# Splitting two weight loads and moving one unit's k^T v forward in the head of a fused retention + mixture-of-experts kernel

## Chip, cores, metric

One NeuronCore of one Trainium2 chip. The metric is the device time of one execution in microseconds (us). The kernel before took 535.12 us in the three runs that came with it (534.94 to 535.67). A line "L576" in a profile is line 576 of that kernel's source. Engines: PE is TensorE, DVE is VectorE, ACT is ScalarE, POOL is GpSimd, SP is SyncE.

## The reference

```python
# q, k, v: (8 batches, 8 heads, 576 positions, 64); w1: (4, 512, 1024); w2: (4, 1024, 512)
scores = q @ k^T / 8                                # per batch and head
ret    = scores * gamma_h ** (i - j)  for i >= j    # decaying causal mask
x      = (ret @ v)  ->  (4608, 512)
out    = sum over 4 experts of  p_e * (relu(x @ w1[e]) @ w2[e])     # p: row-normalised probabilities
```

The kernel computes the retention in chunks of 128 positions (with a remainder chunk of 64). Within a chunk it is a masked product (s, then sT, then o). What comes from earlier chunks is carried as a state k^T v of 64x64 per head (PSUM tile kvp, copied into the SBUF tile sbd).

## The kernel before

The first batch begins with four "units", numbered from 0 (two chunks, that is 256 positions, by 4 heads each). What matters is that each goes through these steps, and that units 1, 2 and 3 follow each other closely in the first 20 us:

```python
def trans_pe(self, between=0):     # PE: 8 transposes into pt; ACT: qkT <- pt   (qkT: a pool of 2 buffers)
    ...
    nc.scalar.activation(self.qk..., pt..., Copy)
def scores(self):                  # PE: 16 small matmuls s <- qkT; DVE: sT <- s * mask
def kv(self):                      # PE: kvp <- k^T v
    kvp = ring_tile("kvp0", [128, 2, 2, 128])
    if hf == 1 and self.carry is None:
        for g in range(2): mm(g, 128, slice(0, 2), 0)   # "prefix", the four 256-wide matmuls
    for g in range(2): mm(g, 128, 1, hf)
    for g in range(2): mm(g, 64, 0, hf)
    ...
    nc.scalar.activation(dst, src, Copy)                # ACT: sbd <- kvp, two of them
def values_own(self):              # PE: o <- sT, v      ("own o")
def values_carried(self):          # PE: o += qkT, sbd   ("carried o"); ACT: xt <- o, two copies

for u in range(NU):
    cast_unit(u + 2)               # ... (the last unit has a part of the first up product ahead of it)
    us[u].values_own()
    us[u + 1].scores()
    us[u].values_carried()
    us[u + 2].trans_pe(1)          # 1: one filler matmul w between the k and the q transposes
    us[u + 1].kv()
```

After this, from about 18 us, come the matmuls of the experts: up products (ph, from xt and w1) and down products (po, from h and w2), first for expert 0. Expert 0's w1 is loaded in two transfers of 512 KB, its w2 in one of 1 MB, all on GpSimd's queue.

## Time and profile before

| | kernel before |
|---|---|
| time, median of 3 | 535.12 us |
| span of the profiled execution | 533.5 us |
| PE busy | 526.2 us, 99% |
| DVE, ACT, POOL busy | 68%, 16%, 28% |
| granted TensorE clock | 1.00 throughout |
| k^T v of unit 1 starts / of unit 3 starts | 12.00 / 16.96 us |

The page's own chain of waits, which is followed back from the last instruction to whatever released each step, is made of PE almost alone (columns: engine, share of the span):

```profile
PE 73%; ACT 2%; DVE 0%; issue 0%
```

In the timeline, a row is a group of instructions of one kind: start, duration, engine, line, operation, out<-in, tile of the PE array, shape, count, and in brackets the idle time just before it and what ended that. The prediction shows the rows of the head.

### The profile page before, as it was taken

The page shows a single profiled execution, that of the slowest core. Times are in us where ns is not written, and L with a number is a line of the kernel's source. Part 1 is how long each engine was busy: PE and PEld are TensorE (multiplying, and loading weights), DVE is VectorE, ACT ScalarE, POOL GpSimd, SP SyncE. Part 2 cuts the span into 40 slices and gives each one's busy share as a digit, 9 for nine tenths or more (in the row PEclk, how much of TensorE's full clock was granted, in tenths as well). Part 3 has the DMA queues.
Part 4 walks back from the last instruction along what each step waited for, and adds up shares of the span by engine and source line. Part 5 has one row for each costly group of instructions (what it writes and reads, how often), then busy time and mean ns, then how long its engine had stood idle before and what let it go on. Part 6 is the DMA issues. An engine that isn't in the chain of part 4 may idle for free.

```text
span 533.5 us, 10230 instructions
## 1 busy us (share of the span) xinstructions
PE 526.2 (99%) x4260; PEld 342.0 (64%) x4260; DVE 361.4 (68%) x456; ACT 85.9 (16%) x175; POOL 146.8 (28%) x189
## 2 busy tenths in 40 slices
PE   8999999999999999999999999999999999999997
PEld 4644544478745985478646865587548844884486
DVE  5436768895577667697578767776765567557763
ACT  4723440012101111020101101100110000000010
POOL 5743104235235334235132514153000000000000
PEclk9999999999999999999999999999999999999999
DMA  9999947867778866736353666454010111110001
GB/s 241 198 217 245 244 122 191 166 154 163 150 166 155 176 142 148 153 83 162 108 135 94 144 139 114 104 118 126 20 41 25 56 39 41 41 41 20 1 24 56
DMA packets 144510, 63.55 MB, mean 119 GB/s; under 512 B 123728, under 2 KB 135264, under 8 KB 144464
## 3 DMA queue, kind: packets, MB, share of 16 engines
q1 hardware_dynamic: 134080, 43.42, 36.1%
q0 software_dynamic: 10240, 19.35, 16.2%
q8 instruction: 33, 0.54, 0.4%
q10 hardware_dynamic: 144, 0.13, 0.1%
q14 instruction: 13, 0.11, 0.1%
HBM read 53.56 MB, written 9.51 MB: 118 GB/s over the span
## 4 chain that ended last, share of the span: by engine, by line
PE 73%; ACT 2%; DVE 0%; issue 0%
PE ph L357 37%; PE pd L469 34%; ACT xt L290 2%; PE o L282 1%; PE o L277 1%; PE py L469 1%; DVE h L363 0%; PE or L342 0%; PE sr L336 0%; PE or L344 0%; DVE ob L497 0%
## 5 line engine op out<-in xcount | busy, mean ns | idle before, releaser
L357 PE MATMUL ph<-xt,w 128*128 128x512 bf16 x1136 | 250.9, 379 | 0.8 <-DVE h L363 0.2
L363 DVE SCALAR_TENSOR_TENSOR h<-ph,pB 128x1024 bf16<-128x1024 f32 x128 | 156.3, 1223 | 58.1 <-PE ph L357 57.2
L357 PEld LDWEIGHTS <-w 128*128 128x128 bf16 x1136 | 109.9, 98 | 127.9
L469 PEld LDWEIGHTS <-h 128*128 128x128 bf16 x1024 | 100.0, 98 | 13.4
L469 PEld LDWEIGHTS <-s 128*128 128x128 bf16 x768 | 75.0, 98 | 8.7
L469 PE MATMUL pd<-wx,h 128*128 128x256 bf16 x512 | 61.1, 273 | 0.2
L469 PE MATMUL pd<-wx,s 128*128 128x256 bf16 x512 | 61.1, 273 | 0.0
L218 POOL DMA_DIRECT2D pB<-pd x28 | 15.7, 562 | 151.7 <-DVE h L363 150.8
L504 POOL TENSOR_TENSOR ob<-v,p 128x256 f32<-128x256 f32 x15 | 11.8, 784 | 111.8 <-DVE v L501 83.8
L237 POOL TENSOR_TENSOR bf_k<-raw_k,gk 128x512 bf16<-128x512 f32 x24 | 26.1, 1088 | 36.6 <-DMA raw_k<-in_k_dram 23.2
L269 DVE TENSOR_TENSOR sT<-s,tri 128x1024 bf16<-128x1024 f32 x24 | 28.2, 1218 | 6.4 <-PE s L267 6.4
L290 ACT ACTIVATE xt<-o 128x768 bf16<-128x768 f32 (+6 forms) x24 | 13.0, 594 | 116.8 <-PE o L282 116.8
L469 PE MATMUL pd<-t4w,h 128*128 128x256 bf16 x256 | 30.6, 273 | 0.0
L442 DVE TENSOR_TENSOR s<-s,h 128x1024 bf16<-128x1024 bf16 x32 | 29.9, 973 | 0.0
L392 PE MATMUL po<-wx,h 128*128 128x512 bf16 x128 | 29.1, 379 | 0.0
L469 PE MATMUL pd<-t2w,s 128*128 128x256 bf16 x240 | 28.7, 273 | 0.0
L469 PE MATMUL pd<-t3w,h 128*128 128x256 bf16 x240 | 28.6, 273 | 0.0
L477 ACT ACTIVATE p<-pd 128x256 f32<-128x256 f32 x16 | 6.1, 383 | 138.8 <-PE pd L469 106.2
L237 POOL TENSOR_TENSOR bf_q<-raw_q,gq 128x512 bf16<-128x512 f32 x24 | 26.6, 1109 | 5.0 <-DMA rawr_v<-in_v_dram 2.1
L446 DVE TENSOR_TENSOR s<-h,s 128x1024 bf16<-128x1024 bf16 x32 | 26.4, 863 | 0.0
L440 DVE TENSOR_TENSOR s<-h 128x1024 bf16<-128x1024 bf16 x32 | 23.7, 779 | 0.0
L486 DVE TENSOR_TENSOR u<-pd,p 128x256 f32<-128x256 f32 x15 | 6.4, 424 | 22.4 <-PE pd L469 22.3
(160 smaller groups left out, 376.4 us busy)
## 6 DMA issues: line engine op xcount, KB each, us to landing
pB<-pd POOLq DMA_DIRECT2D x28, 256.0 KB, 3.6
raw_k<-in_k_dram SPq DMA_DIRECT2D x48, 128.0 KB, 2.6
raw_q<-in_q_dram SPq DMA_DIRECT2D x48, 128.0 KB, 2.9
raw_v<-in_v_dram SPq DMA_DIRECT2D x48, 128.0 KB, 3.3
wx<-in_moe_w_dram POOLq DMA_DIRECT2D x4, 1024.0 KB, 14.5
out_dram<-oa SPq DMA_DIRECT2D x16, 256.0 KB, 2.4
out_dram<-ob SPq DMA_DIRECT2D x15, 256.0 KB, 2.2
w<-in_moe_w_dram POOLq DMA_DIRECT2D x3, 1024.0 KB, 13.8
```

Source lines behind the costliest of these rows:

```text
L218: eng.dma_start(out=pB[t, e], in_=pd[e:e + 1, t * NT:(t + 1) * NT].to_broadcast([128, NT]))
L237: eng.tensor_tensor(bfs[p % 2][n], raw1[n], g[:, :, 2 * p:2 * p + 2].unsqueeze(3).to_broadcast([128, NC, 2, D]), op=MULT)
L269: nc.vector.tensor_tensor(sT[:, :, :, :].rearrange("p j c t -> p (j c) t"), s[:, :, :, :].rearrange("p j c t -> p (j c) t"), tri[:, :].uns ...
L290: nc.scalar.activation(xt_of(t)[:, self.ps, n0 + a - t * NT:n0 + z - t * NT], o[:, :, a:z], Copy)
L357: nc.tensor.matmul(ph[:, f, :], lhsT=w1_sb[e][:, dc, fc * 128:(fc + 1) * 128], rhs=x[:, dc, :], start=(dc == 0), stop=(dc == NDC - 1))
L363: nc.vector.scalar_tensor_tensor(h[:, fk:fk + 2, :], ph, 0.0, pB[t, e][:, :].unsqueeze(1).to_broadcast([128, 2, NT]), op0=MAX, op1=MULT)
L392: nc.tensor.matmul(po[:, g, :], lhsT=h[:, e * NFC + fc, ns * 128:(ns + 1) * 128], rhs=wx[e // 2][:, (e % 2) * NFC + fc, :, :].rearrange("p ...
L440: nc.vector.tensor_tensor(self.alloc("s1")[:, l], h[:, l, self.b], h[:, r, self.b], op=ADD)
L442: nc.vector.tensor_tensor(self.alloc("s2")[:, l], self.s1[:, l], h[:, l, self.a], op=SUB)
L446: nc.vector.tensor_tensor(self.alloc("s4")[:, l], h[:, r, self.a], self.s2[:, l], op=SUB)
L469: mm = nc.tensor.matmul(dst, lhsT=src[:, kk, tok], rhs=rhs(c), start=(start and c == 0), stop=(c == KH - 1), skip_group_check=True)
L504: nc.gpsimd.tensor_tensor(self.ob[:, HF:Dm], self.v, self.p5, op=ADD)
```

## The change

The intent has two parts. Smaller weight pieces let the first up and down products start with a part of the weights. And k^T v of unit 2 is used to fill PE's waits in unit 1: its prefix runs directly after unit 1's k^T v, into the second bank of the same PSUM tile; its other eight matmuls run before the carried o of unit 1, which used to wait for ACT. Its two state copies go from ACT to DVE, and the filler matmul between unit 3's transposes is dropped. The diff, cut to its core:

```diff
@@ the weights
-    load_w1_at = {1: (0, slice(0, F // 2)), 2: (0, slice(F // 2, F))}
+    load_w1_at = {1: (slice(0, F // 4),), 2: (slice(F // 4, F // 2), slice(F // 2, F))}
-    load_w2(0)
+    load_w2(0, 0, NFC // 2)
+    load_w2(0, NFC // 2, NFC)
@@ first down products of expert 0: fc 0-3 of two token blocks, then fc 4-7 of both
+        if e == 0 and m == 0:
+            todo = [(gg, fc) for gg in range(2) for fc in range(4 * g, 4 * g + 4)]
@@ kv(): tile of two banks, prefix on its own, copies
+                self.kvt = ring_tile("kvp0", [128, 2, 2, 2, 128])
-                    nc.scalar.activation(dst, src, Copy)
+                    self.reads.append(nc.vector.tensor_copy(dst, src) if others else nc.scalar.activation(dst, src, Copy))
@@ the loop over units
         us[u].values_own()
         us[u + 1].scores()
+        if u == 1:
+            us[2].kv(False, us[1].reads)
         us[u].values_carried()
-            us[u + 2].trans_pe(1)
-        if u + 1 < NU:
+            us[u + 2].trans_pe(1 - u)
+        if u in (0, 2):
             us[u + 1].kv()
+        if u == 0:
+            us[2].kvt = us[1].kvt
+            us[2].kv_open(1)
+            us[2].kv_front(us[1].reads)
```

(`others` lists the reads of unit 1's bank; they are declared independent of the writes to unit 2's bank.)

## The prediction

> **What bounds the kernel now.** I read the page first (shares of the span, then the costliest groups), then the stretches of time, then the timeline of the head, engine by engine. The page says that this is a TensorE kernel:
>
> ```profile
> span 533.5 us, 10230 instructions
> PE 526.2 (99%) x4260; PEld 342.0 (64%) x4260; DVE 361.4 (68%) x456; ACT 85.9 (16%) x175; POOL 146.8 (28%) x189
> ```
>
> A busy PE alone proves little, so I looked where it is not busy. The windows show that all edited code runs in the first stretch, and that the second has no hole at all:
>
> ```profile
> 0.00:20.00 20.00, 17.36 (x244) 10.33 (x245) 11.70 (x31) 11.02 (x22) 12.25 (x29) 1.00 1.02 225
> 20.00:70.00 50.00, 50.00 (x340) 24.55 (x339) 26.11 (x60) 23.24 (x37) 17.60 (x25) 1.00 1.06 216
> ```
>
> The third figure is PE's busy time: 17.36 of 20 us, then 50.00 of 50. From about 17 us on the kernel is one dense stream of matmuls. A gain or loss of PE time in the head should therefore arrive at the end undiminished, unless a load becomes late. The timeline of PE there, where units 1 to 3 of the first batch (score s, own values o, carried values o from sbd, transposes pt, k^T v as kvp) hand work to ACT and DVE and back:
>
> ```profile
> 12.00 0.72 PE L576 MATMUL kvp<-bf_v,bf_k 128*128 128x128 bf16 x8
> 12.87 0.42 PE L611 MATMUL o<-sT,bf_v 64*64 64x128 bf16 x16
> 13.33 0.42 PE L558 MATMUL s<-qkT 64*64 64x128 bf16 x16
> 13.99 0.28 PE L621 MATMUL o<-qkT,sbd 128*128 128x128 bf16 x2 [0.24 <-ACT sbd L596]
> 14.11 0.39 PE L535 MATMUL pt<-ident,bf_k 128*128 128x128 bf16 x4
> 14.33 0.38 PE L136 MATMUL w<-zz 128*128 128x512 bf16 x1
> 14.55 0.39 PE L535 MATMUL pt<-ident,bf_q 128*128 128x128 bf16 x4
> 14.77 1.15 PE L576 MATMUL kvp<-bf_v,bf_k 128*128 128x256 bf16 x12
> 15.85 0.42 PE L611 MATMUL o<-sT,bf_v 64*64 64x128 bf16 x16
> 16.11 0.42 PE L558 MATMUL s<-qkT 64*64 64x128 bf16 x16
> 16.46 0.66 PE L621 MATMUL o<-qkT,sbd 128*128 128x128 bf16 x4
> 16.96 1.15 PE L576 MATMUL kvp<-bf_v,bf_k 128*128 128x256 bf16 x12
> ```
>
> The printed durations overlap; starts are what counts. From the individual starts in narrow windows: 0.056 us between 128-wide matmuls, 0.109 between 256-wide, 0.216 between 512-wide, and about 0.148 instead of 0.056 where the tile shape changes (64x64, 64-row, 128-row). Taking those steps out, PE waits 0.22 us before o at 12.87 (for sT of DVE), 0.21 before s at 13.33 (qkT), 0.30 before the carried o at 13.99 (sbd), and 0.26 inside the four matmuls from 16.46 (sbd again). That is 0.99 us of waiting in units 1 and 2, plus one filler matmul w of 0.216. ACT in the same time:
>
> ```profile
> 12.26 1.02 ACT L537 ACTIVATE qkT<-pt 128x1024 bf16<-128x1024 bf16 x1
> 13.18 0.76 ACT L596 ACTIVATE sbd<-kvp 64x256 bf16<-64x256 f32 x2
> 14.31 0.77 ACT L637 ACTIVATE xt<-o 128x256 bf16<-128x256 f32 x2 [0.38 <-PE o L621]
> 15.03 1.02 ACT L537 ACTIVATE qkT<-pt 128x1024 bf16<-128x1024 bf16 x1
> 15.96 0.77 ACT L596 ACTIVATE sbd<-kvp 64x256 bf16<-64x256 f32 x2
> ```
>
> The reader should see that the qkT of unit 3 (15.03 to 16.05) begins as soon as the xt copies of unit 1 end, and that s at 16.11 follows it by 0.05.
>
> **What the Trainium skill says.** "PSUM — Partial Sum Buffer", section "Engine vs sequencer instructions": the queues of ScalarE and VectorE are strict FIFO. The trace agrees: the sbd copy at 13.18, whose kvp was complete at about 12.7, stands behind the qkT at 12.26. The same page, "PSUM bank collisions raise a hardware error", wants two engines on different banks; the shared kvp tile keeps to that (unit 1 in the first bank, unit 2 in the second), so PE may fill one while ACT empties the other. No run yet shows it. "TensorEngine Tiling (Array Packing)", "Key Properties": changing the tiling mode drains the TensorE; the trace shows it as the extra 0.09 us per change of shape. "TensorE: Matmul & The Clock Gate", "What's actually happening": an idle window of about 3.4 us halves the clock; no wait here is near that and the granted clock is 1.00, so the removed filler is not needed for it.
>
> **The change, part by part.** *Weights.* The first half of expert 0's w1 becomes two pieces, the second of which is issued with the other half; w2 becomes two pieces, and the first pair of down products takes fc 0 to 3 of both token blocks before fc 4 to 7. The transfers in question, issue to landing:
>
> ```profile
> w<-in_moe_w_dram POOLq DMA_DIRECT2D x1, 512.0 KB, 7.9
> w<-in_moe_w_dram POOLq DMA_DIRECT2D x1, 512.0 KB, 7.7
> wx<-in_moe_w_dram POOLq DMA_DIRECT2D x1, 1024.0 KB, 10.5
> ```
>
> With issues at 9.76, 12.50 and 15.03 they land at 17.6, 20.2 and 25.5. PE first uses them at 18.04, 22.22 and 25.68, starting each time without a hole. So the loads arrive only 0.2 to 0.4 us before PE wants the first and third: nothing to gain by itself, but the split buys room. The queue is in order and full; each 512 KB takes 2.6 us. By that I estimate landings near 16.2, 17.7, 20.3, 23 and 25.6, against uses at 18, 19.6, 22.2, 25.7 and 27.4: at least 1.8 us spare each. Two more issues on POOL, 0.8 us each, fall into waits or ahead of table work that nobody wants before 20 us. Worth: 0.
>
> *k^T v of unit 2.* Its 12 matmuls move. The four 256-wide ones (the prefix, from unit 0) run right after unit 1's kvp, the other eight after unit 2's scores; the filler between the transposes of unit 3 is gone. The two ACT copies (0.77 us) become two DVE copies. For those I take the sbd additions of L593 later in the trace, the same 64x256 shape, 0.41 us each: 0.8 us for both. Now the timeline by hand, with the steps above. kvp of unit 1 has its last start at 12.505. Prefix: 12.65 to 12.98. Own o of unit 1: 12.98 + 0.20 = 13.18 (before 12.87; sT has long been there). s of unit 2: 13.44 (before 13.33; no wait for qkT, which ends at 13.28). The eight kvp matmuls: 13.79, last start 14.30. Carried o of unit 1: 14.44 (before 13.99; sbd is ready at 13.94, so no wait). Transposes: 14.57, last start 14.96, result at 15.18. So all three waits are filled with work, as intended.
>
> But the carried o is 0.46 us later, and ACT works in order. xt of unit 1 starts at 14.51 + 0.22 + 0.04 = 14.77 instead of 14.31, and qkT of unit 3, which stands behind it, at 15.49 instead of 15.03; it ends at 16.51. Own o of unit 2 needs its PSUM buffer, which that xt frees at 15.53: it starts at 15.60, after 0.50 of waiting (sT of DVE, 15.46, is there just before). s of unit 3 then waits for qkT until 16.51 + 0.05 = 16.56 (before 16.11): another 0.70. The DVE copies run from 15.46 to 16.27 and are in time; the carried o of unit 2 goes at 16.91 without a wait, and kvp of unit 3 at 17.15. Before it was at 16.96.
>
> The sum, to check: waits 0.50 + 0.70 = 1.20 instead of 0.99, two more changes of shape (0.19), filler gone (-0.22): +0.18 to +0.19 us. The ACT copies that were removed stood behind qkT, not ahead of it, so they do not bring qkT forward. From 17 us on nothing waits, in the original neither, so the shift stays: 535.12 + 0.19 = 535.3 us.
>
> **The rivals.** *First: the intended gain.* If the wait for sbd goes and nothing takes its place, PE saves up to 0.99 + 0.22 - 0.19 = 1.0 us, making 534.1. For it: the copies do leave the busy ACT, and all waits of unit 1 are filled. Against it: qkT of unit 3 hangs on xt of unit 1 through ACT's order, and the profile has that pair back to back already. It would need xt or qkT to start some 0.4 us sooner than I work out. A part of it (534.8) is possible, if my steps at changes of shape are too long. *Second: the smaller pieces are slower.* The quarters of w1 have rows half as long; if they cost half as much again, 0.7 to 1.3 us more, everything behind them in the queue lands later. For it: the queue is full until 70 us. Against it: 1.8 us or more is spare at each first use, and PE shows no load wait later. It would make 535.3 to 536. *Third: DVE becomes late*, with the copies delaying sT of unit 3. Against it: that score ends near 17.0, the copies near 16.3; worth 0 unless a copy took over 0.75 us.
>
> **Range and chances.** Everything at stake is within about 1 us of 535, that is 0.2%, and the three runs before already spread over 0.73 us. I put the main line at 535.3, the gain at 534.1 to 534.8 and slow loads at up to 536; 534.5 to 536.0 should hold it 8 times in 10. Two per cent would be 10.7 us, and the whole head in which anything moves waits less than 3 us in all: same 0.98, either side 0.01.
>
> **What would show it.** In the timeline of the changed kernel: kvp of unit 1 as one run of 12 from 12.0; the carried o of unit 1 near 14.44 without a wait on sbd; xt near 14.77 and qkT near 15.49; s of unit 3 near 16.56 with ACT qkT as releaser of some 0.7 us idle; kvp of unit 3 near 17.15 and the first ph near 18.23. DVE's two copies should take 0.8 us between the masks of units 2 and 3. The first po should follow ph densely near 25.87. If s of unit 3 starts before 16.2, the main step is wrong and the time falls below 535. If PE waits for a DMA of w or wx, the second rival holds. If the head is as I say and the total differs by more than 0.5 us, something after 70 us moved that I have not seen.

## The result

The changed kernel took 535.45 us in the median (535.03 to 535.66, six runs), the kernel before beside it 535.47 us (534.94 to 536.39, six runs). The ratio is 0.9996, with a 95% interval of 0.9983 to 1.0009: the same. A ratio here is the mean time of one kernel's fast runs over that of the other's in the same rounds, so it isn't quite the ratio of the medians.

The page of the changed kernel, span and busy times, and then its windows, whose third figure is PE's busy time:

```profile
span 534.0 us, 10194 instructions
PE 523.8 (98%) x4220; PEld 341.9 (64%) x4259; DVE 362.3 (68%) x458; ACT 85.3 (16%) x173; POOL 147.3 (28%) x191
```

```profile
0.00:20.00 20.00, 16.95 (x242) 9.97 (x244) 11.85 (x24) 10.23 (x20) 13.06 (x29) 1.00 1.04 221
20.00:70.00 50.00, 49.68 (x335) 24.70 (x339) 26.74 (x64) 23.36 (x36) 18.11 (x27) 1.00 1.08 218
```

PE's smaller busy time is not a gain. The changed kernel has 4259 weight loads but only 4220 matmul records, where the kernel before has 4260 of each: some 40 matmul records are missing from this trace. The 49.68 in the second window is for the same reason no hole: 335 matmuls for 339 weight loads. Starts of instructions are safe to compare, sums of busy time are not.

The timeline of PE in the head of the changed kernel:

```profile
11.97 1.27 PE L582 MATMUL kvp<-bf_v,bf_k 128*128 128x128 bf16 x12
13.17 0.42 PE L625 MATMUL o<-sT,bf_v 64*64 64x128 bf16 x16
13.42 0.39 PE L563 MATMUL s<-qkT 64*64 64x128 bf16 x16
13.74 0.72 PE L582 MATMUL kvp<-bf_v,bf_k 128*128 128x128 bf16 x8
14.40 0.28 PE L635 MATMUL o<-qkT,sbd 128*128 128x128 bf16 x2
...
15.66 0.42 PE L625 MATMUL o<-sT,bf_v 64*64 64x128 bf16 x16 [0.53 <-DVE sT L565]
16.41 0.42 PE L563 MATMUL s<-qkT 64*64 64x128 bf16 x16 [0.33 <-ACT qkT L542]
...
16.99 1.15 PE L582 MATMUL kvp<-bf_v,bf_k 128*128 128x256 bf16 x12
```

The first five rows have no bracket: unit 1 waits for nothing any more. The waits now stand in unit 2: its own o waits for DVE, and the scores of unit 3 wait for ACT. The last row, k^T v of unit 3, starts at 16.99, where it was 16.96. The ACT and DVE rows behind it:

```profile
14.72 0.76 ACT L651 ACTIVATE xt<-o 128x256 bf16<-128x256 f32 x2 [0.81 <-PE o L635]
15.33 1.02 ACT L542 ACTIVATE qkT<-pt 128x1024 bf16<-128x1024 bf16 x1
```

```profile
15.43 0.84 DVE L610 CAST sbd<-kvp 64x256 bf16<-64x256 f32 x2
```

The spans of the two profiled executions differ by 0.47 us (533.96 and 533.49, from the trace). This can be split into three terms, and I use the same three for every run below: the start of unit 1's k^T v ("head start"); the **chain** from there to the start of unit 3's k^T v, which holds all the edited PE work; and the **rest** up to the end.

| us | head start | chain | rest | sum |
|---|---|---|---|---|
| before | 12.00 | 4.96 | 516.53 | 533.49 |
| changed | 11.97 | 5.02 | 516.97 | 533.96 |
| difference | -0.03 | +0.06 | +0.44 | +0.47 |

So the edited code costs 0.06 us, and most of the rest comes from one place far away. The chain of waits of the changed kernel, in order of time, between 165 and 174 us (columns: start, duration, what):

```profile
166.93 5.68 DMA qTr<-bfr_q
172.61 0.14 issue
172.75 0.28 PE sr L337 x4
```

The first scores of a remainder chunk (sr) wait for a transposing DMA (qTr) that SP issues. In the kernel before sr starts 155.32 us after unit 3's k^T v; here it starts 155.75 after. That is the +0.44, to 0.01. (The profiled execution of the changed kernel is the slowest of its six, so this delay need not be typical of the other five.) The bracket that the timeline puts there says only 0.27, because the modelled end of the matmul ahead covers the rest. The row before and after:

```profile
172.28 0.28 PE L336 MATMUL sr<-qTr,kTr 128*128 128x64 bf16 x4
172.75 0.28 PE L337 MATMUL sr<-qTr,kTr 128*128 128x64 bf16 x4 [0.27 <-DMA qTr<-bfr_q]
```

More on this below.

### The profile page after: what moved, and what is told of

It reads as the page before. It is cut to its first block, busy times and chain, and to the rows that moved or that the text cites. A ratio compares the mean times of both kernels' runs of the same rounds, so it can differ in the third digit from the quotient of the medians.

```text
span 534.0 us, 10194 instructions
## 1 busy us (share of the span) xinstructions
PE 523.8 (98%) x4220; PEld 341.9 (64%) x4259; DVE 362.3 (68%) x458; ACT 85.3 (16%) x173; POOL 147.3 (28%) x191
## 4 chain that ended last, share of the span: by engine, by line
PE 72%; ACT 2%; DMA 1%; issue 0%; DVE 0%; POOL 0%; POOLq 0%
PE ph L358 35%; PE pd L474 34%; ACT xt L291 2%; PE o L283 1%; DMA qTr<-bfr_q 1%; PE o L278 1%; PE py L474 1%; DVE h L364 0%; PE or L343 0%; PE sr L337 0%; PE or L345 0%; POOL bf_k L238 0%; DVE ob L502 0%; PE kvp L254 0%; POOLq L238 0%
## 5 line engine op out<-in xcount | busy, mean ns | idle before, releaser
L451 DVE TENSOR_TENSOR s<-h,s 128x1024 bf16<-128x1024 bf16 x32 | 25.6, 838 | 0.0
```

Of the source, the lines that this page charges most:

```text
L451: nc.vector.tensor_tensor(self.alloc("s4")[:, l], h[:, r, self.a], self.s2[:, l], op=SUB)
```

## The experiments

Theory A, formed from the two traces: the waits that the change fills come back in unit 2. The eight k^T v matmuls stand on PE ahead of the carried o and of unit 3's transposes, so xt (ACT) and the transposes are both later; ACT works in order, qkT of unit 3 comes behind both, and PE waits for it. Rival B: something else makes up the time (the split, the copies on DVE, PSUM buffers). All twelve runs were correct. Single looks have the state "unknown", as one run alone gives no comparison; their granted clock was 1.00 (0.999 in one) except where said. A total of a single look means little here: the head start alone ranged from 11.67 to 12.65 us over the fourteen profiled executions. The chain is the steady quantity: 5.020, 5.020 and 5.023 us in three executions whose PE order in it is that of the changed kernel (e3 has only fillers in its waits), and 4.961 and 4.962 in two with the order of before. It isn't fixed by the order alone: e1 and e7, also of one order, are 0.05 apart.

| run | head start | chain | rest | time, us |
|---|---|---|---|---|
| before | 12.00 | 4.96 | 516.53 | 535.20 |
| changed | 11.97 | 5.02 | 516.97 | 535.66 |
| e1_kv_late | 12.10 | 4.64 | 516.55 | 535.02 (median of 6: 535.36) |
| e2_fill_before | 12.65 | 5.46 | 516.93 | 536.74 |
| e3_fill_after | 11.96 | 5.02 | 516.55 | 535.23 |
| e4_act_copies | 12.26 | 5.66 | 518.29 | 537.94 |
| e5_no_split | 11.84 | 5.02 | 516.55 | 535.10 |
| e6_split_only | 11.71 | 4.96 | 516.70 | 535.08 |
| e7_late_no_split | 12.27 | 4.59 | 516.55 | 535.11 |
| e8_dve_only | 11.67 | 5.12 | 516.55 | 535.05 |
| e9_act_copies_fill | 12.38 | 5.59 | 516.80 | 536.50 |
| e10_act_copies_again | 11.68 | 5.60 | 516.94 | 535.92 |
| e11_qkt_first | 11.95 | 4.92 | 516.55 | 535.11 |
| e12_late_act | 12.13 | 4.83 | 517.05 | 535.70 |

### e1: the eight k^T v matmuls behind the transposes

```diff
-        if u == 1:
-            us[2].kv(False, us[1].reads)
         us[u].values_carried()
         if u + 2 < NU:
             us[u + 2].trans_pe(1 - u)
+        if u == 1:
+            us[2].kv(False, us[1].reads)
```

> The changed kernel, with only the place of unit 2's last eight k^T v matmuls altered: after the carried o of unit 1 and the transposes of unit 3, instead of before them. Theory A (the order of ACT sets it: carried o of unit 1, then xt, then qkT of unit 3, then s of unit 3): the carried o goes back to about 13.96, as soon as sbd is there; xt starts near 14.28, qkT near 14.9 (held by the transposes, which wait for bf_q until 14.4), s of unit 3 near 15.99 instead of 16.41, k^T v of unit 3 near 16.57 instead of 16.99. So 0.42 us less in the head, and about 0.4 us (0.08%) less in all: 535.0 where the kernel before has 535.4. Theory B (sT of DVE for unit 2 sets the head, ending at 15.51): own o of unit 2 stays at 15.66 in both, and k^T v of unit 3 stays at 16.99, no change. Theory C (what the head gains is lost later on waits for transfers): the head gains as in A, but the first ph or po waits for weights, or the wait for qTr near 172 us grows, and the total does not follow.

The chain fell to 4.64 us, 0.38 less than in the changed kernel and 0.32 less than before. PE's timeline there:

```profile
15.79 0.42 PE L625 MATMUL o<-sT,bf_v 64*64 64x128 bf16 x16 [0.28 <-DVE sT L565]
16.13 0.42 PE L563 MATMUL s<-qkT 64*64 64x128 bf16 x16
16.48 0.42 PE L635 MATMUL o<-qkT,sbd 128*128 128x128 bf16 x4
16.74 1.15 PE L582 MATMUL kvp<-bf_v,bf_k 128*128 128x256 bf16 x12
```

Counted from the head start, own o of unit 2 stands where it was (3.69 us in both), and s of unit 3 comes 0.40 us sooner; so sT of DVE isn't what paces the head (theory B of the expectation). The page shows no wait of s for qkT any more. By starts it has shrunk from 0.50 to 0.09 us: s still follows the end of qkT, at 16.08, by 0.05. What holds qkT here is PE's transposes, and what holds the q transposes is DVE's cast of unit 3's q (it ends at 14.51, they start at 14.56), which had waited for its load. Five rounds gave 535.36 us (six runs, 535.02 to 535.73) against 535.58 for the kernel before (eleven runs, 535.06 to 537.33), ratio 0.9992 (0.9979 to 1.0006). So A holds for the head, while 0.3 us (0.06%) is too little to be resolved in the total. This is the best placement tried with both parts of the change, and it isn't shown to beat either kernel.

### e2 and e3: two filler matmuls before the carried o, or after the transposes

```diff
         if u == 1:
             us[2].kv(False, us[1].reads)
+            warm(2)                               # e2: 2 x 0.216 us of PE work
         us[u].values_carried()
         if u + 2 < NU:
             us[u + 2].trans_pe(1 - u)
+        if u == 1: warm(2)                        # e3: here instead
```

> The changed kernel plus two filler matmuls (0.216 us each) just before the carried o of unit 1. Theory A: everything on the chain moves by the full 0.43: carried o near 14.83 (14.40), xt 15.15, qkT 15.76, s of unit 3 16.84 (16.41), k^T v of unit 3 17.42 (16.99), although PE has 0.86 us of waiting behind that place. Theory B: the filler falls into the wait for sT, own o of unit 2 stays at 15.66 and k^T v of unit 3 at 16.99.

> The same two fillers, but after the transposes of unit 3, before own o of unit 2. (They take a PSUM buffer that the xt copies free at about 15.48, so they cannot start sooner.) Theory A: own o of unit 2 is 0.4 us later, near 16.06, but s of unit 3 still starts with qkT near 16.41 and k^T v of unit 3 near 16.99: 0.43 us of work for nothing. Theory B (own o of unit 2 paces the head): s and k^T v of unit 3 move by 0.4, to 16.8 and 17.4.

In e2 the chain took 5.46 us, 0.44 more than in the changed kernel: two fillers of 0.216 arrive in full, and s of unit 3 waits the longer for qkT:

```profile
17.53 0.42 PE L563 MATMUL s<-qkT 64*64 64x128 bf16 x16 [0.83 <-ACT qkT L542]
```

The total of 536.74 overstates this, since its head began 0.68 us later than that of the changed kernel. In e3 the same two fillers (one of their two records is missing) cost nothing:

```profile
15.53 0.38 PE L137 MATMUL w<-zz 128*128 128x512 bf16 x1 [0.41 <-ACT xt L651]
16.05 0.42 PE L625 MATMUL o<-sT,bf_v 64*64 64x128 bf16 x16
16.40 0.42 PE L563 MATMUL s<-qkT 64*64 64x128 bf16 x16
16.75 0.40 PE L635 MATMUL o<-qkT,sbd 128*128 128x128 bf16 x4
```

Own o of unit 2 starts later, at 16.05, and s of unit 3 still at 16.40 with no wait shown before it, chain 5.02. So work ahead of the carried o counts in full, and 0.43 us of work between the transposes and s is free: what s waits for hangs on the former.

### e4, e10, e9: the state copies of unit 2 on ACT

```diff
-    self.reads.append(nc.vector.tensor_copy(dst, src) if others else nc.scalar.activation(dst, src, Copy))
+    self.reads.append(nc.scalar.activation(dst, src, Copy))
```

> The changed kernel with the third part undone: the two sbd copies of unit 2 on ACT again (L610). In ACT's order they now stand before xt of unit 1, so theory A: they run from 14.5 to 15.3, xt starts near 15.2 instead of 14.72, qkT near 15.8, s of unit 3 near 16.89 and k^T v of unit 3 near 17.47, 0.48 us later than in the changed kernel. If the engine of these copies is of no account (theory B), k^T v of unit 3 stays near 16.99.

In e4 the two copies stand on ACT ahead of xt and qkT, and the chain grew from 5.02 to 5.66 (+0.64, where A had said +0.48), with 0.99 us of idle before s of unit 3. But the total rose to 537.94, more than the chain explains. The windows of e4, whose column before the last two is the granted clock:

```profile
18.00:21.00 3.00, 3.00 (x20) 2.05 (x18) 1.71 (x12) 1.53 (x4) 2.62 (x10) 0.50 1.21 189
```

The TensorE clock was halved just after the waits, from about 17.8 to 21.2 us. I took "waiting lets the clock drop" for a third theory, and ran the same kernel again, and once more with five fillers in the waits (two after the transposes, three before s of unit 3).

> A repeat of the version with unit 2's sbd copies on ACT, whose first run had the TensorE clock at half from 17.8 to 21.2 us. If the long waits of PE from 15.1 to 17.3 cause that, it comes again, starting between 17 and 20 us, with a loss of about 1.7 us; if it was chance, the clock stays at 1.00 and unit 3's k^T v comes 5.55 us after unit 1's.

> The same version with five filler matmuls inside those waits: two before own o of unit 2, three before s of unit 3. They end before qkT is there, so s of unit 3 keeps its place (5.0 us after unit 1's k^T v). If lack of PE work is what halves the clock, the clock stays at 1.00 and unit 3's k^T v comes near 5.5; the time is then some 1.7 us below that of the run with the half clock. If not, the clock falls here too.

The same window in e10:

```profile
18.00:21.00 3.00, 3.00 (x44) 2.39 (x43) 1.64 (x17) 1.76 (x5) 2.62 (x10) 1.00 1.24 204
```

No drop, with the same idle of 0.99 us before s. The chain is 5.60; the 0.06 that e4 has more lies after the start of its s, where its clock began to be halved. In e9 the clock stayed at 1.00 as well, with a chain of 5.59, so the fillers cost nothing. As the drop didn't come back without fillers, e9 doesn't show that fillers prevent it. One of two executions of this kernel lost 1.50 us to the clock: the first po starts 10.22 us after unit 3's k^T v in e4 and 8.72 after it in every other run. The other 0.25 of its longer rest is a wait for qTr. What decides the drop stays open. What e9 and e10 show is that DVE copies are needed for this placement: on ACT they cost 0.57 to 0.58 us of chain at the full clock.

### e5, e6, e7: the split of the weights taken away, or alone

e5 is the changed kernel and e7 is e1 with the loads and the order of the down products as before; e6 is the kernel before with these edits alone.

```diff
-    load_w1_at = {1: (slice(0, F // 4),), 2: (slice(F // 4, F // 2), slice(F // 2, F))}
+    load_w1_at = {1: (slice(0, F // 2),), 2: (slice(F // 2, F),)}
-    load_w2(0, 0, NFC // 2)
-    load_w2(0, NFC // 2, NFC)
+    load_w2(0)
-        if e == 0 and m == 0:
+        if False:
```

> The changed kernel with its first part undone: expert 0's w1 in two halves, w2 in one piece, the first down products in the old order. All stretches counted from the start of unit 1's k^T v, since that start itself moved between 11.96 and 12.65 us from run to run. If the split is worth nothing here: unit 3's k^T v 5.02 us later, as in the changed kernel, the three landings near 17.6, 20.2 and 25.5, and no or at most 0.1 us of waiting at the first po. If the smaller pieces cost queue time (the second piece of w2 landed between 25.3 and 26.3 in four runs): the whole w2 lands at 25.5 or sooner. If the split was needed at the changed kernel's pace: PE waits over 0.1 us for wx.

> The kernel before with only the split of the weights and the new order of the first down products. Expected: the head as before (4.96 us from unit 1's k^T v to unit 3's), no wait for w or wx, landings as in the changed kernel (15.8, 17.0, 20.1, 23 to 24, 25.3 to 26.3), so no change of the time. If the pieces were too slow, a wait for w at the first ph (18.0) or its second half (19.6) would show.

> The version with unit 2's k^T v after the transposes (4.64 us to unit 3's k^T v) without the split of the weights. PE then comes to the first po 0.3 us sooner than in the kernel before, near 25.35, while w2 in one piece lands near 25.5. If the split is there to buy this room: a wait of 0.1 to 0.3 us for wx at the first po. If the split is of no account: no wait there, and the same 4.64.

The chain doesn't see the split: 5.02 without and 5.02 with it for the changed order, 4.96 and 4.96 for the order of before. For the order of e1 it is 4.59 without (e7) and 4.64 with it (e1): the load of unit 3's q landed 1.62 us after the head start in e7 and 1.69 after it in e1, and the q transposes begin 0.06 after the cast of that q in both. One execution each doesn't show whether the split makes that difference. PE starts po without a hole in all of them. The totals (535.10, 535.08, 535.11, and 535.38 for the kernel before beside them) don't tell the kernels apart. The chain of e7 is the shortest of all.

### e8: only the DVE copies

```diff
+                elif hf == 1 and self.g == 0:
+                    nc.vector.tensor_copy(dst, src)      # kernel before, otherwise unchanged
                 else:
                     nc.scalar.activation(dst, src, Copy)
```

> The kernel before with only the two sbd copies of unit 2 on DVE, k^T v at its old place. DVE is idle from 15.46, k^T v ends at 15.92, so the copies run from about 15.97 to 16.82 instead of 15.96 to 16.73 on ACT. The carried o of unit 2 still waits for them; unit 3's k^T v comes 5.04 us after unit 1's (4.96 before). If the copies on ACT had been what held the head, it should come sooner than 4.9.

The chain grew by 0.16 us, to 5.12, twice the 0.08 that I had expected. In the old order DVE is no better placed than ACT: there the copies took 0.86 us from 15.71, where ACT took 0.77, and the carried o waits for them:

```profile
16.62 0.34 PE L623 MATMUL o<-qkT,sbd 128*128 128x128 bf16 x3 [0.25 <-DVE sbd L596]
```

So this part is worth something only together with the earlier k^T v.

### e11: unit 3's transposes, and so its qkT, ahead of the carried o of unit 1

```diff
         if u == 1:
             us[2].kv(False, us[1].reads)
+            us[3].trans_pe(0)
         us[u].values_carried()
-        if u + 2 < NU:
+        if u + 2 < NU and u != 1:
             us[u + 2].trans_pe(1 - u)
```

> The changed kernel, with the transposes of unit 3 and so its qkT copy issued ahead of the carried o and the xt copies of unit 1. Theory A (ScalarE's order is what delays qkT: in the changed kernel it starts 0.23 us after the transposes would allow): transposes from 14.45, qkT starts at about 15.10 instead of 15.33 and ends at 16.12, xt of unit 1 slides to about 16.0. If no PSUM buffer waits for that xt, s of unit 3 starts at about 16.17 instead of 16.41 and the chain from k^T v of unit 1 to that of unit 3 takes about 4.78 us instead of 5.02. If o of unit 2 or s of unit 3 needs the buffer that xt frees, it starts only at about 16.85, with ACT xt as releaser, and the chain takes 5.3 to 5.7. Rival (qkT is held by something other than the order of ScalarE's queue): qkT stays near 15.33 after the start of the head, s near 16.4, chain near 5.0. All times for a k^T v of unit 1 at 11.97; to be shifted with it. Total within 0.7 us of the kernel before in any case.

The timelines of ACT and of PE:

```profile
15.20 1.02 ACT L542 ACTIVATE qkT<-pt 128x1024 bf16<-128x1024 bf16 x1 [1.32 <-PE o L635]
```

```profile
16.28 0.42 PE L563 MATMUL s<-qkT 64*64 64x128 bf16 x16 [0.56 <-ACT qkT L542]
```

Chain 4.92: the direction of A, but 0.10 us of gain (5.02 to 4.92) where I had expected 0.24. qkT started 0.10 us after the time I had given. The bracket names a reason: it waits for the carried o of unit 1. Releasers are inferred, but the code bears this one out: qkT has two buffers, unit 3's is that of unit 1, and the carried o of unit 1 is its last reader. I had overlooked this. The rival (qkT stays near 15.33) is refuted, and xt of unit 1, now at 16.12, held nobody up.

### e12: e1 with the copies on ACT

The edit is e4's, made in e1.

> The variant with unit 2's k^T v behind the transposes, with its state copies back on ScalarE. Theory A: the copies stand behind qkT of unit 3 there, as in the kernel before (qkT start + 0.92 to + 1.70), and the carried o of unit 2 waits for them inside its four matmuls by about 0.25 us; k^T v of unit 3 follows the start of qkT by 1.93 as in the kernel before, chain 4.89 us instead of 4.64. Rival (the copies' engine matters only for the early placement): no such wait, chain 4.64. Total: not to be told apart from the kernel before.

Chain 4.83, against 4.89 by A and 4.64 by the rival. The copies ran at 15.96 behind qkT, and the second of the four matmuls of the carried o waited for them. With the late placement the DVE copies are worth 0.18 us.

## Why the prediction was right or wrong

**The total was right** (535.3 predicted, 535.45 measured, 534.5 to 536.0 as the range), and so was its core: the waits move rather than go. The total alone proves little, as the kernel before measured 535.47 beside it and the six runs of each kernel spread over 0.6 and 1.5 us; that the head was right is read from the starts.

**The filled waits: right, to 0.05 us.** Predicted and measured starts: own o of unit 1 13.18 and 13.17; s of unit 2 13.44 and 13.42; the eight k^T v 13.79 and 13.74; carried o of unit 1 14.44 and 14.40, with no wait. The DVE copies took 0.84 us (0.8 predicted) and were in time. PE wrote the second bank from 13.74 while ACT was still copying unit 1's state out of the first (to 13.91), and all outputs were correct. The first po followed densely, at 25.71 (25.87 predicted).

**The new waits: the mechanism right, the size about 0.1 us too large, and one step of it wrong.** With the prediction's own method (gap between starts less the step that a dense sequence takes), own o of unit 2 waited 0.745 - 0.148 = 0.60 us and s of unit 3 waited 0.550 - 0.055 = 0.50. That is 1.10 instead of 0.50 + 0.70 = 1.20. (The prediction had own o released by xt's PSUM buffer, with sT just before it; in the trace sT ends at 15.51 and xt at 15.48, so the two are as close as it had said. As e3 shows, own o had time to spare in any case.) With two more changes of shape (0.19) and without the filler (0.22), 1.10 - 0.99 + 0.19 - 0.22 = +0.08; the chain measured +0.06, against +0.19 predicted. The failing step is the sentence that "the qkT of unit 3 (15.03 to 16.05) begins as soon as the xt copies of unit 1 end". It put the delay of qkT wholly on ACT's order and moved it by the full 0.46 us of the carried o. In the kernel before, qkT was really held by the transposes: their last start there is 14.717, and qkT begins 0.316 us later; in e11, where the carried o at 14.885 is the last to be waited for, it is 0.316 as well. In the changed kernel the last transpose starts at 14.912, which would allow 15.23, and qkT began at 15.33, 0.29 after the start of the second xt copy. Counted from the head start qkT is 0.32 us later than before: 0.22 because PE does the transposes later, 0.10 because xt stands ahead of it in ACT's queue. Both follow from the same placement, so the conclusion stood.

**Which rival came closest.** The intended gain (534.1) did not come; e1 shows why, and that a third of it was to be had in the head: with the eight matmuls behind the transposes the chain is 0.32 us shorter than before. "DVE becomes late" did not come in the changed kernel, but did in e8.

**Smaller pieces: slack right in sign, wrong in size.** The estimates for the pieces were 16.2, 17.7, 20.3, 23 and 25.6; they landed at 15.79, 16.97, 20.09, 23.93 and 26.32 in the profiled run. fc 4 to 7 are first needed eight matmuls after po begins, at 25.71 + 8 x 0.216 = 27.4, so 1.1 us was spare there, not 1.8; in e6 the same piece landed at 26.80, po began at 25.39, and only 0.3 was left. The load behind it, w1 of expert 1, landed at 31.34 (30.43 before). No PE wait came of it.

**Not foreseen: qTr, far from the edits.** The prediction said that a total off by over 0.5 us would mean something after 70 us that it had not seen; the total was off by less, yet there is such a thing. Counted from unit 3's k^T v, sr starts at 155.32 or 155.33 if nothing holds it. qTr landed at 154.00 to 154.96 in the four profiled kernels without the split (before, e5, e7, e8), and at 155.02 to 155.70 in nine of the ten with it, whatever the order of the head; the tenth, e4, had its clock halved and can't be compared. In six of these nine the rest is 0.15 to 0.5 us longer; in e1, e3 and e11 qTr was just in time. SP issues its loads up to qTr in the same order in all fourteen traces. What tells e6 from the kernel before is two more transfers on GpSimd's queue and the order of the first down products. So in these traces the split goes together with a later qTr, and it may cost more than the head's 0.06 us. That it is the cause was not shown. The margin between the groups is 0.06 us with one execution per kernel. The record puts e5 to e8 on one chip, e1 to e4 and e9 to e12 on two others, so that among the experiments only e6 is a case with the split on the same chip as cases without it. The timed rounds, with a scatter of 0.6 to 2.3 us, can't confirm it. How two more transfers, issued before 17 us, would act at 172 us stays open too. What the traces do show is that qTr is late with its whole queue: in each of the fourteen it lands 0.2 to 0.4 us after kTr, which SP issues just before it, behind six loads and beside a transfer of GpSimd's (pB).

## What to carry to other kernels

When work is moved into a wait, ask which engines' next inputs are produced behind it: here twelve matmuls filled three waits and delayed the transposes and copies on which the next unit hung, so that 0.99 us of waiting in units 1 and 2 went and 1.10 us came back around units 2 and 3. The better place was behind the producer of that input (e1), and the way to find it was to put dummy work at each candidate place and see where it is free (e2 and e3). And when the quantity in question is 0.1% of the time, compare starts inside the trace rather than totals: the chain repeated within 0.01 us for two orders of instructions and within 0.05 for a third, while the start of the head moved by up to 1 us from run to run.

## What the Trainium skill lacked or had wrong

- "TensorEngine Tiling (Array Packing)", "Key Properties", says that a change of tiling mode drains the TensorE, without a size. Here a start-to-start step is 0.148 us across a change of shape and 0.056 us without one, so 0.09 us each; the changed kernel has two more.
- "TensorE: Matmul & The Clock Gate", "What's actually happening", ties the halved clock to an idle window of about 3.4 us, free-running. In e4 the clock was 0.50 from 18 to 21 us although PE had been busy for 1.56 of 2.00 us (14 to 16) and 1.01 of 2.00 (16 to 18), with a longest shown wait of 0.99 us; e10, the same kernel with 1.25 and 1.31 us busy in these windows, kept 1.00. How much idle inside a window is enough isn't stated, and these two runs don't settle it.
- I found no page that says how long a small transposing DMA takes beside other traffic. For qTr near 167 us it was 4.0 to 5.7 us from issue to landing over the fourteen traces, with an identical order on the issuing queue. Most of that is not the transfer's own: the qTr of the changed kernel that was issued at 89.54 us landed 2.30 us later.
